# Four small edits of order in a fused linear-attention and gated-FFN kernel: fill-in matmuls of the head, one conversion step, the place of a square, the place of a joint insertion

## The chip, the cores and the metric

The kernel runs on one core of a Trainium2 chip. A core has five engines that run side by side, each with a queue of its own that it works through strictly in order: TensorE (PE, the matmuls, with its weight loads shown as PEld), VectorE (DVE), ScalarE (ACT), GpSimd (POOL) and SyncE (SP, which here only issues DMAs). They meet by semaphores. The metric is device time in microseconds for one execution; lower is better. An instruction that waits for another engine blocks everything behind it in its own queue, and this is what most of this document turns on.

## The reference: what is computed

For 8 batches, 8 heads, 576 positions and head size 64:

```
kv  = einsum('bhsd,bhse->bhde', k, v)
out = einsum('bhsd,bhde->bhse', q, kv)
x   = out / sqrt(mean(out*out, -1) + 1e-6) * g_norm      -> (4608, 512)
y   = (sigmoid(x @ w_gate) * (x @ w_val)) @ w_out        d_ff = 1536
```

All arithmetic is in float32. The three weight matrices arrive as float64, so the kernel gets them as 64-bit words and turns these into float32 itself.

## The kernel before, in words

**Chunks.** The 4608 tokens are worked off in nine chunks of 512 (`G`). Chunk 0 uses ordinary matmuls: eleven blocks of `plain` (line 630, matmuls at L618) after one block that is woven into the head, then the second layer (`second`, L853). Chunks 1 to 8 use a fast matrix multiplication with 26 products for each 4-by-4 grid of blocks (`PRODUCTS1`, `PRODUCTS2`): `first_layer_fast` (L977) runs 78 products, numbered p = 0 to 77, in three groups of 26, and `second_layer_fast` (L1079) runs 26 more with three matmuls each. Each product adds into one of up to eleven named regions; there are five PSUM banks for them, handed out and taken back in the queue `free`.

**Head.** The first four pairs of heads (batch 0) go through `attention` before chunk 0. Their steps are named in a string, `order` (L651), and issued in that order on all engines: `KVn` (matmuls, L299), `KVOn` (DVE copy, L303), `Qn` (transposes on PE, L309), `QOn` (ACT copy, L314), `Un` (matmuls, L326), `SQn` (ACT square, L331), `SUMn` (DVE, L335), `ROOTn` (ACT, L339), `NORMn` (DVE, L343 and L345), `Xn` (transposes on PE, L353), `XOn` (ACT, L362). Between them stand `warmN`: N matmuls of 128 by 128 into a bank that nobody reads (L671). In float32 each such matmul is two instructions in the profile. Their operand is `ident`, the identity that GpSimd makes first (masks.py:197 and 199). `wN` issues loads of weights and `cU.S`, `aU.S` are steps of a conversion.

**Conversion.** A unit u of weights (18 in all: units 0 to 11 for the first layer, 12 to 17 for the second) is turned into float32 by five DVE steps `s0` to `s4` (L195, L210, L222, L226, and L233 or L235) and two ACT steps: `a0` (L200) runs behind `s0`, and `s2` (L222) needs it; `a1` (L215) runs behind `s1`, and `s3` needs it. `s4` and `s2` also issue loads for a later unit on SP. In chunk 0 the next step is taken whenever `CV` stands in the string `places` (L827), at a place counted in matmuls of chunk 0 (eight to a block); an `s0` or `s1` brings its ACT step with it. During the second layer of chunk 0 three of four matmuls take one step each.

**The end of a block of chunk 0.** Each block's sigmoid (`gate`, ACT, L623) and its product with the other half (`end`, DVE, L626) are put off by `late` and issued at places 0 and 2 of the next block. At a place, `late` comes before the steps of `places`.

**Joint insertions.** Batches 1 to 7 are attended four pairs of heads at a time (`feed`), in two runs for each batch. A run's matmuls (`u_mm`, L450, and in front of the first run `kv_mm`, L389 and L400) are put between products of the fast layer as one block: the joint insertion. It lands in the three-bank tile `at` and in one lent bank. `u_square` (`q0`, `q1` in the strings) copies the lent piece over (L456), gives the bank back, and squares the whole (L459), both on ACT. Sums (`s00`, L462), root (`r0`, L465) and norms follow. The strings at L518 to L523 give, for each step, the product p behind which it is issued; the first string is for chunk 1 (`b == 2`), the second for chunk 2 (`b == 3`), the third for chunks 3 to 6. Behind a product come first its own sums and copies (`combine`, L943 for a copy on ACT, L947 for sums on DVE), then the steps of the string.

One dependence matters for the change: in the list of products, region B is copied out by ACT behind product i = 5 of each group of 26, and product i = 6 adds into that region, so it must wait for the copy:

```
("A", 24, 14, "o4=C"),  ("C", 26, 16, "o3=B o1=A"),  ("B", 25, 19, "o1=o1+B")     i = 4, 5, 6
```

Of the kernel before, what the change touches and what calls it, by code (L numbers as in the profile page):

```python
# [10 lines left out]
FP32 = mybir.dt.float32  # L11
# [9 lines left out]
def kernel(  # L21
# [11 lines left out]
    nc = tc.nc  # L33
# [4 lines left out]
    P = 128  # L38
# [34 lines left out]
    const = ctx.enter_context(tc.tile_pool(name="const", bufs=1))  # L73
# [75 lines left out]
    def load_unit(u, halves=(0, 1)):  # L149
        if u >= len(units):  # L150
            return
        kind, f = units[u]
        if 0 in halves:
            staged[u] = raw.tile([P, 2, DM], I64, tag="st", name="st", bufs=NST)
        st = staged[u]
        for i in halves:
            if kind == "gv":
                src = (moe_w_gate, moe_w_val)[i].rearrange("(m p) f -> p m f", p=P)[:, :, P * f:P * f + P]
                nc.sync.dma_start(out=st[:, i].rearrange("p (m f) -> p m f", m=NMT), in_=src)
            else:  # L160
                nc.sync.dma_start(out=st[:, i], in_=moe_w_out[P * (f + i):P * (f + i) + P, :])
# [7 lines left out]


    EXP_OFF = 896
    one = const.tile([P, 1], FP32, name="one")
    nc.vector.memset(one, 1.0)
    exp_off = const.tile([P, 1], FP32, name="exp_off")
    nc.vector.memset(exp_off, -EXP_OFF * 2.0 ** 23)

# [83 lines left out]
    w1 = const.tile([P, N3, 4 * NMT, 2, P], FP32, name="w1")  # L260
    w2 = const.tile([P, NFT, DM], FP32, name="w2")
    ident = const.tile([P, P], FP32, name="ident")
# [111 lines left out]
    def feed(b):  # L374
# [132 lines left out]
        u0, u1 = heads_run(0), heads_run(1)  # L507
# [5 lines left out]
        if b == 1:  # L513
# [2 lines left out]
        names = f"t00 t01 t10 t11 u0 q0 s00 s01 r0 {n_.format(0)} x00 x01 u1 q1 s10 s11 r1 {n_.format(1)}".split()  # L516
        steps_ = dict(zip(names, t0 + t1 + u0 + u1[:-2]))
        where = """0:t00 5:t01 25:u0 26:q0 28:t10 30:s00,s01 33:t11 35:r0 36:n00 37:n01 39:n02 40:n03 42:n04 43:n05 44:n06  # L518
                   51:x00 52:x01 53:u1 56:q1 57:s10,s11 60:r1 62:n10,n11 63:n12 65:n13 66:n14 68:n15 69:n16""" if b == 2 else """
                   5:t00 8:t01 25:u0 29:t10 30:q0 33:s00,s01 36:r0 39:t11 41:n00 47:n01 51:x00,x01 54:u1  # L520
                   56:q1,s10,s11 61:r1 64:n10 66:n11""" if b == 3 else """
                   3:t00 7:t01 25:u0 28:t10 30:q0,s00,s01 37:r0 39:t11 47:n00,n01 53:x00,x01 54:u1
                   56:q1,s10,s11 60:r1 61:n10 63:n11"""  # L523
        first = [(int(w_.split(":")[0]), steps_[x]) for w_ in where.split() for x in w_.split(":")[1].split(",")]
        return kv, first, u1[-2:]
# [53 lines left out]
    def bank(i):  # L579
        return (psum_mm if i < 2 else psum).tile([P, 512], FP32, tag=f"mm{i}", name="mm")  # L580
# [19 lines left out]
    warm, pair_kv = bank(0), bank(1)  # L600
# [29 lines left out]
    def plain(c, u, ps, steps_at):  # L630
# [18 lines left out]


    order = """  # L651
        w1 w2 warm8 KV0 Q0 KVO0 QO0 warm4 U0 SQ0 KV1 Q1 SUM0 ROOT0 KVO1 QO1 NORM0 warm3 U1 SQ1 X0 XO0 SUM1 ROOT1
        c0.0 a0.0 c0.1 a0.1 NORM1 warm11 X1 XO1 c0.2 KV2 Q2 KVO2 QO2 c0.3 c0.4 w3 warm3 U2 SQ2 KV3 Q3 SUM2 ROOT2 KVO3 QO3
        NORM2 b0.0.0 U3 SQ3 b0.1.0 X2 XO2 c1.0 SUM3 ROOT3 a1.0 c1.1 a1.1 NORM3 b0.0.1 b0.1.1 b0.0.2 X3 XO3 b0.1.2
        c1.2 c1.3 c1.4 w4 b0.0.3 b0.1.3
    """
# [1 line left out]
    for token in order.split():  # L658
        name = token.rstrip("0123456789.")
        n = [int(i) for i in token[len(name):].split(".")]  # L660
        f = n[0]
        if name == "b":
            blk = blk or Plain(0, F_ORDER[0], (warm, pair_kv))
            blk.mm(n[1], n[2])
        elif name in ("c", "a"):
            conversion[f][name][n[1]]()
        elif name == "w":
            load_unit(f)
        elif name == "warm":
            for _ in range(f):  # L670
                nc.tensor.matmul(warm[:, 0:P], ident, ident, start=True, stop=True)  # L671
        else:
            a[f][steps[name]]()
            if token == f"Q{NE - 1}":
                first_ctx.__exit__(None, None, None)
                hp = ctx.enter_context(tc.tile_pool(name="hp", bufs=1))
                h_main = [hp.tile([P, 4 * NT, P], FP32, name=f"h{j}") for j in range(N3)]
                h_more = hp.tile([P, N3, 3 * NT, P], FP32, name="h_more")
# [122 lines left out]
    def w1_form(c, j, part, v):  # L801
        if c == 1:
# [10 lines left out]
    w1_more[1] = [more[:, i] for i in range(10, 18)] + [sgs[-1][:, GH * i:GH * i + GH] for i in range(2)]  # L813
    spare_sg = sgs.pop()
    batch1, second_batch = feed(1), feed(2)
    named = {"LL": lambda: load_late(1), "LL2": lambda: load_late(2), 
             "W0": lambda: w1_sums(0), "W1": lambda: w1_sums(1),
# [6 lines left out]
    for i, which in enumerate("ab"):  # L824
# [3 lines left out]
        1:CV,CV 2:CV,Q0 4:CV,CV 5:CV,CV 6:CV,LL 7:CV,CV 10:CV,CV 11:Q1 15:CV 16:CV,CV 17:t00  # L828
        18:CV,CV 19:t01 22:CV,CV 25:CV 26:CV,CV 29:au,LL2 30:CV
        31:asq 32:CV,t10,as0,as1,art 34:arc,CV,an0 35:CV 36:CV,t11,an1 37:an2 38:CV 40:CV,CV 41:CV,ax0  # L830
        43:ax1 44:bu 46:CV,W0 47:bsq,ASIDE 48:CV,CV 50:CV,bs0 52:CV,CV 54:bs1 55:CV,CV,brt,D 57:CV,CV 58:CV 60:CV,brc
        62:bn0,bn1 63:bn2 64:CV 65:CV,CV,CV 66:CV,CV 67:CV 71:bx0 72:CV 74:W1 75:bx1
        80:CV,CV,CV,CV,CV 84:CV 87:CV
    """
    at_place = {}
    for some in places.split():
# [311 lines left out]
    X1 = (18, 19, 20, 21, 22, 22, 23, 23, 24, 24, 25, 26, 28, 30, 31, 33, 35, 37)  # L1148
# [59 lines left out]
```

## Time and profile before

| what | value |
|---|---|
| median of three runs | 999.95 us (999.59 to 1000.1) |
| profiled execution: its own time | 1001.39 us |
| profiled execution: its span | 999.6 us |
| PE busy | 992.4 us (99%) |
| DVE / ACT / POOL busy | 719.1 / 343.0 / 616.2 us |
| head, until PE runs on without a break | 0 to 33.1 us |
| first layer of chunk 0 | 33.1 to 116.2 us |
| second layer of chunk 0 | 116.2 to 158.1 us |
| chunk 1 | 158.1 to 262.0 us |
| chunks 2 to 6 | 106.3 us each, to 793.7 us |
| chunks 7 and 8 | 101.0 us each |

The span runs from the first to the last instruction. A row of the timeline gives the start, the duration, the engine and source line, the operation with output and inputs, how many instructions were merged, and in brackets how long the engine stood idle before and what released it. Matmuls are pipelined, so the end of a row reaches past the start of the next; the distance of two starts says more than a duration.

### The profile page before, as it was taken

The numbers are of one execution on the slowest core, as the hardware profiler recorded it, in microseconds if no ns is written. First come the engines' busy times: TensorE is split into PE (matmuls) and PEld (weight loads), VectorE is DVE, ScalarE is ACT, GpSimd is POOL, SyncE is SP. The second block draws the span as 40 slices with busy tenths as digits, with TensorE's granted clock in tenths as the row PEclk, the third lists the DMA queues.
The fourth block names the chain that finished last, engine by engine and source line by source line (L and its number), as shares of the span: only waits on it lengthen the run. The fifth ranks groups of instructions, "written<-read, shape, count | busy, mean of one in ns | idle before, by whom it ended". The sixth has DMA issues, their size and how long they took to land.

```text
span 999.6 us, 16578 instructions
## 1 busy us (share of the span) xinstructions
PE 992.4 (99%) x5958; PEld 816.2 (82%) x5958; DVE 719.1 (72%) x1185; ACT 343.0 (34%) x621; POOL 616.2 (62%) x991
## 2 busy tenths in 40 slices
PE   8999999999999999999999999999999999999998
PEld 7455447888888888888888888888888888888887
DVE  4989999898758766784777576866587566755672
ACT  4566332561144213530344124511442123213320
POOL 0439997798259634865286708771686349744963
PEclk9999999999999999999999999999999999999999
DMA  9995515763889468746975677656854455444614
GB/s 270 275 262 176 174 53 142 220 225 104 289 277 276 158 190 272 205 159 198 280 226 161 187 221 260 176 172 188 282 179 145 152 182 203 158 148 165 215 51 123
DMA packets 149522, 194.96 MB, mean 195 GB/s; under 512 B 79840, under 2 KB 121696, under 8 KB 149440
## 3 DMA queue, kind: packets, MB, share of 16 engines
q0 software_dynamic: 22512, 116.41, 35.1%
q1 hardware_dynamic: 120848, 75.66, 26.7%
q10 hardware_dynamic: 6080, 1.84, 0.8%
q8 instruction: 47, 0.77, 0.3%
q14 instruction: 35, 0.29, 0.1%
HBM read 160.04 MB, written 25.56 MB: 186 GB/s over the span
## 4 chain that ended last, share of the span: by engine, by line
PE 93%; DVE 4%; issue 1%; ACT 1%; DMA 0%; SPq 0%; DVEq 0%; ACTq 0%
PE mm L977 54%; PE mm L1079 27%; PE mm L618 5%; PE mm L853 3%; PE at L450 2%; DVE cz L226 1%; DVE w L222 1%; DVE w L195 1%; PE at L400 1%; PE mm L400 1%; DVE cz L210 0%; DMA q<-in_q_dram 0%; PE two L326 0%; DVE w L235 0%; DVE h L626 0%
## 5 line engine op out<-in xcount | busy, mean ns | idle before, releaser
L977 PE MATMUL mm<-xs,w 128*128 128x256 f32 x1428 | 331.8, 380 | 0.0
L977 PEld LDWEIGHTS mm<-xs,w 128*128 128x128 f32 x1428 | 270.5, 190 | 37.9 <-ACT sg L943 1.2
L977 PE MATMUL mm<-xT,w 128*128 128x256 f32 x948 | 230.6, 380 | 0.0
L977 PEld LDWEIGHTS mm<-xT,w 128*128 128x128 f32 x948 | 179.5, 190 | 25.0 <-issue 0.5
L799 POOL DMA_DIRECT2D w<-kept x84 | 46.9, 559 | 203.6 <-PE mm L977 200.1
L947 DVE TENSOR_TENSOR sg<-sg,mm 128x512 f32<-128x512 f32 (+1 forms) x176 | 100.8, 599 | 75.1 <-PE mm L977 34.4
L1079 PE MATMUL mm<-w,h 128*128 128x256 f32 x630 | 142.8, 379 | 0.0
L1079 PEld LDWEIGHTS mm<-w,h 128*128 128x128 f32 x630 | 119.7, 190 | 16.3
L943 ACT COPY temps<-mm 128x512 f32<-128x512 f32 (+1 forms) x128 | 66.2, 540 | 184.7 <-PE mm L1079 94.7
L939 POOL TENSOR_TENSOR h<-h,sg 128x512 f32<-128x512 f32 x72 | 96.8, 1362 | 43.9 <-ACT sg L936 27.8
L752 POOL TENSOR_TENSOR h<-h 128x128 f32<-128x128 f32 x216 | 109.9, 521 | 16.6 <-DVE h_more L752 13.1
L1079 PE MATMUL mm<-w,h_more 128*128 128x256 f32 x474 | 108.2, 379 | 0.0
L936 ACT ACTIVATE sg<-sg 128x512 f32<-128x512 f32 x96 | 59.7, 630 | 127.3 <-DVE sg L947 127.3
L1079 PEld LDWEIGHTS mm<-w,h_more 128*128 128x128 f32 x474 | 90.1, 190 | 12.2
L943 ACT COPY sg<-mm 128x512 f32<-128x512 f32 (+1 forms) x112 | 56.5, 511 | 84.1 <-PE mm L1079 45.3
L752 POOL TENSOR_TENSOR h_more<-h 128x128 f32<-128x128 f32 x120 | 58.5, 491 | 34.8 <-DVE h L939 30.5
L947 DVE TENSOR_TENSOR temps<-temps,mm 128x512 f32<-128x512 f32 (+1 forms) x96 | 59.5, 620 | 27.1 <-PE mm L1079 16.8
L947 DVE TENSOR_TENSOR temps<-mm,temps 128x512 f32<-128x512 f32 (+1 forms) x64 | 39.8, 623 | 52.3 <-PE mm L1079 23.9
L618 PE MATMUL mm<-xT,w 128*128 128x512 f32 x176 | 77.2, 595 | 0.1
L943 ACT COPY h<-mm 128x512 f32<-128x512 f32 x48 | 28.1, 586 | 142.9 <-PE mm L977 142.9
L947 DVE TENSOR_TENSOR sg<-mm,sg 128x512 f32<-128x512 f32 (+1 forms) x64 | 39.7, 620 | 42.4 <-PE mm L1079 21.9
L618 PEld LDWEIGHTS mm<-xT,w 128*128 128x128 f32 x176 | 32.8, 190 | 40.0 <-issue 36.8
(154 smaller groups left out, 1298.1 us busy)
## 6 DMA issues: line engine op xcount, KB each, us to landing
w<-kept POOLq DMA_DIRECT2D x42, 896.0 KB, 5.1
w<-kept POOLq DMA_DIRECT2D x90, 384.0 KB, 4.5
w<-kept POOLq DMA_DIRECT2D x42, 768.0 KB, 5.0
out_dram<-sg SPq DMA_DIRECT2D x119, 64.0 KB, 1.7
q<-in_q_dram SPq DMA_DIRECT2D x96, 72.0 KB, 5.1
xT<-xTs SPq DMA_DIRECT2D x96, 72.0 KB, 4.6
st<-in_moe_w_gate_dram SPq DMA_DIRECT2D x12, 512.0 KB, 5.3
st<-in_moe_w_val_dram SPq DMA_DIRECT2D x12, 512.0 KB, 6.6
```

What stands on the lines that cost most here:

```text
L400: nc.tensor.matmul(ps[m][HD * g:HD * g + HD, e], mains[2 * m + g, "k"][:, c], mains[2 * m + g, "v"][:, c], start=(b == 2 and e == 0 and j ...
L450: nc.tensor.matmul(to[HD * e:HD * e + HD], qTs[HD * g:HD * g + HD, c:c + HD], kvq[HD * g:HD * g + HD, m, e], start=True, stop=True)
L618: nc.tensor.matmul(self.ps[i], w[("wg", "wv")[i], self.f][:, m, :], xT[self.c][:, m, :], start=(m == 0), stop=(m == NMT - 1), skip_group_c ...
L752: ops.append((eng, lambda v=v, x=x, sign=sign, y=y, eng=eng: eng.tensor_tensor(out=h_form(v, j), in0=h_form(x, j), in1=h_form(y, j), op=op ...
L799: nc.gpsimd.dma_start(out=granule(g)[:, 0:n], in_=kept1[g // NPA % N3, g % NPA][:, 0:n])
L853: nc.tensor.matmul(ps[t], gv[0, f][:, P * t:P * t + P], w["wo", f], start=(f == 0), stop=(f == NFT - 1), skip_group_check=True)
L936: nc.scalar.activation(out=o["o" + step[1]], in_=o["o" + step[1]], func=AF.Sigmoid)
L939: mult.tensor_tensor(out=o[x], in0=o[x], in1=o[y], op=ALU.mult)
L943: nc.scalar.copy(out=o[out_], in_=o[expr])
L947: tt(out=o[out_], in0=o[x], in1=o[y], op=ALU.add if sign == "+" else ALU.subtract)
L977: nc.tensor.matmul(regions[name][1][:, g], ws[:, g], xf[c][wv], start=(new and g == 0), stop=True, skip_group_check=True)
L1079: nc.tensor.matmul(regions[name][1], h_form(hv, j), ws[:, j], start=(used[i] and j == 0), stop=(j == N3 - 1), skip_group_check=True)
```

## The change

1. Head: the fill-in matmuls multiply a tile of ones with itself. That tile is set by one DVE memset of 128 by 128 (it was 128 by 1; the old name stays as its first column, the bias of `a0`). Their numbers change: 9 for 8 at the start, one more between `KV0` and `Q0`, 3 for 4 ahead of `U0`, one between `SQ0` and `KV1`, 14 for 11 ahead of `X1`.
2. Conversion in chunk 0: a third step at place 48, none at place 87; the steps in between each move up by one in the sequence. At place 48 the additional step is `s4` of unit 8 (L233).
3. Chunks 2 to 6: the square of the first run is issued at product 26, right behind the insertion at 25, instead of at product 30.
4. Chunk 1: the second run's insertion comes behind product 54 instead of 53.

In chunk 0 the order on DVE and ACT from the additional step on is, for the three blocks that the prediction speaks of (numbers in brackets are lines; u is the unit):

```
DVE before: ... [226 u8] [626] [233 u8] [462] [195 u9] ...
DVE after:  ... [226 u8] [233 u8] [626] [195 u9] [462] ...
DVE before: [222 u10] [498] [226 u10] [233] [195 u11] [210 u11] [626] [222 u11] [226 u11]
DVE after:  [222 u10] [226 u10] [498] [233] [195 u11] [210 u11] [222 u11] [626] [226 u11]
ACT before: [494 x18] [623] [200 u11] [215 u11] [623] [200 u12] [623] [215 u12]
ACT after:  [494 x18] [623] [200 u11] [215 u11] [200 u12] [623] [215 u12] [623]
```

The order on SP and on GpSimd stays as it was. The diff:

```diff
-    one = const.tile([P, 1], FP32, name="one")
-    nc.vector.memset(one, 1.0)
+    ones = const.tile([P, P], FP32, name="ones")
+    nc.vector.memset(ones, 1.0)
+    one = ones[:, 0:1]
...
-                   51:x00 52:x01 53:u1 56:q1 57:s10,s11 60:r1 62:n10,n11 63:n12 65:n13 66:n14 68:n15 69:n16""" if b == 2 else """
-                   5:t00 8:t01 25:u0 29:t10 30:q0 33:s00,s01 36:r0 39:t11 41:n00 47:n01 51:x00,x01 54:u1
+                   51:x00 52:x01 54:u1 56:q1 57:s10,s11 60:r1 62:n10,n11 63:n12 65:n13 66:n14 68:n15 69:n16""" if b == 2 else """
+                   5:t00 8:t01 25:u0 26:q0 29:t10 33:s00,s01 36:r0 39:t11 41:n00 47:n01 51:x00,x01 54:u1
                    56:q1,s10,s11 61:r1 64:n10 66:n11""" if b == 3 else """
-                   3:t00 7:t01 25:u0 28:t10 30:q0,s00,s01 37:r0 39:t11 47:n00,n01 53:x00,x01 54:u1
+                   3:t00 7:t01 25:u0 26:q0 28:t10 30:s00,s01 37:r0 39:t11 47:n00,n01 53:x00,x01 54:u1
...
-        w1 w2 warm8 KV0 Q0 KVO0 QO0 warm4 U0 SQ0 KV1 Q1 SUM0 ROOT0 KVO1 QO1 NORM0 warm3 U1 SQ1 X0 XO0 SUM1 ROOT1
-        c0.0 a0.0 c0.1 a0.1 NORM1 warm11 X1 XO1 c0.2 KV2 Q2 KVO2 QO2 c0.3 c0.4 w3 warm3 U2 SQ2 KV3 Q3 SUM2 ROOT2 KVO3 QO3
+        w1 w2 warm9 KV0 warm1 Q0 KVO0 QO0 warm3 U0 SQ0 warm1 KV1 Q1 SUM0 ROOT0 KVO1 QO1 NORM0 warm3 U1 SQ1 X0 XO0 SUM1 ROOT1
+        c0.0 a0.0 c0.1 a0.1 NORM1 warm14 X1 XO1 c0.2 KV2 Q2 KVO2 QO2 c0.3 c0.4 w3 warm3 U2 SQ2 KV3 Q3 SUM2 ROOT2 KVO3 QO3
...
-                nc.tensor.matmul(warm[:, 0:P], ident, ident, start=True, stop=True)
+                nc.tensor.matmul(warm[:, 0:P], ones, ones, start=True, stop=True)
...
-        43:ax1 44:bu 46:CV,W0 47:bsq,ASIDE 48:CV,CV 50:CV,bs0 52:CV,CV 54:bs1 55:CV,CV,brt,D 57:CV,CV 58:CV 60:CV,brc
+        43:ax1 44:bu 46:CV,W0 47:bsq,ASIDE 48:CV,CV,CV 50:CV,bs0 52:CV,CV 54:bs1 55:CV,CV,brt,D 57:CV,CV 58:CV 60:CV,brc
         62:bn0,bn1 63:bn2 64:CV 65:CV,CV,CV 66:CV,CV 67:CV 71:bx0 72:CV 74:W1 75:bx1
-        80:CV,CV,CV,CV,CV 84:CV 87:CV
+        80:CV,CV,CV,CV,CV 84:CV
```

## The prediction

> **What bounds the kernel.** I read the page's chain that ended last first, then the PE timeline stretch by stretch for starts that lie further apart than they need, then the waits of PE's weight loads, then the other engines around each late start. PE carries the span:
>
> ```profile
> PE 93%; DVE 4%; issue 1%; ACT 1%; DMA 0%; SPq 0%; DVEq 0%; ACTq 0%
> ```
>
> So an edit pays only where PE itself is late. That is in the head (busy 29.97 of its first 33.10 us) and in a few places behind it. The head, PE alone:
>
> ```profile
> 1.37 3.78 PE L671 MATMUL mm<-ident 128*128 128x128 f32 x16 [1.37 <-POOL ident masks.py:199]
> 5.08 1.55 PE L299 MATMUL mm<-v,k 96*64 96x64 f32 x24
> 6.82 1.19 PE L309 MATMUL two<-ident,q 96*128 96x96 f32 x6 [0.19 <-DMA q<-in_q_dram]
> 7.80 1.97 PE L671 MATMUL mm<-ident 128*128 128x128 f32 x8
> 9.70 1.29 PE L326 MATMUL two<-kvq,qTs 64*64 64x64 f32 x40
> 10.93 0.92 PE L299 MATMUL mm<-v,k 96*64 96x64 f32 x24
> 11.78 0.71 PE L309 MATMUL two<-ident,q 96*128 96x96 f32 x6
> 12.33 0.86 PE L671 MATMUL mm<-ident 128*128 128x128 f32 x6
> ```
>
> The same work is slow at first and fast later: KV 1.55 then 0.92, Q 1.19 then 0.71, fill-ins 0.213 us apart then 0.112. TensorE runs at half speed until about 10.8 us. And U0 (9.70) starts a whole us after its input is ready (the copy L314 runs 8.05 to 8.69), because four fill-ins stand before it.
>
> The weight loads show the two other places that the change touches:
>
> ```profile
> PEld mm L853 <- DVE w L235: 1.7, 2, 1.0
> PEld mm L977 <- ACT sg L943: 1.4, 6, 0.2
> ```
>
> L853: at 123.10 and 130.37 PE waits for a converted unit. The L853 matmuls start at 116.21 and are 0.429 apart; 32 of them need 13.73 us, but the third unit starts after 14.16, and each of the two waits is followed by one start that is 0.10 late: 0.53 in all.
>
> L977: the six waits are one each in chunks 1 to 6, six products behind an insertion. Chunk 3, PE and then ACT:
>
> ```profile
> 397.05 4.59 PE L977 MATMUL mm<-xs,w 128*128 128x256 f32 x20
> ```
> ```profile
> 397.99 1.13 ACT L459 ACTIVATE sqs<-at 128x1152 f32<-128x1152 f32 x1
> 399.01 1.07 ACT L943 COPY sg<-mm 128x512 f32<-128x512 f32 x2
> ```
>
> The square holds up the copy of region B until 399.6, just when product i = 6 wants to add into it. Twenty matmuls at 0.216 plus the 0.17 of a row's tail are 4.48; the row has 4.59, so the wait costs 0.10.
>
> **The change, part by part.** The sum is made against the profiled execution's own span, 999.6; it lay 0.35 below the median of the runs shown (999.95; with the profiler on, the execution itself took 1001.39). I subtract from the median.
>
> *Head.* A memset of 128 by 128 took 0.20 on POOL, one of 128 by 1 0.06 on DVE; taking 0.20 (same shape), ones are there at 0.81 + 0.20 and PE starts at 1.06 instead of 1.37. Two more instructions at 0.213 put KV0 at 5.2 (5.08 before); its operands no longer wait for anything. The pair behind KV0 (0.43) lies in the gap 6.5 to 6.82, in which PE waits for q. So PE works from 1.06 on with no gap above 0.15, where before 0.14 and about 0.4 were free between 4.9 and 6.8. I take it that full speed comes before Q0, since before it came at the end of the first stretch as dense as this (7.0 to 10.8). Then: Q0 at 6.82 (its DMA binds) for 0.71, copy 0.04 later for 0.64, U0 at 8.25; the three fill-ins (0.86 with tail, from 7.38) are through by then. From a fast U's start to its square is 0.88 (13.54 to 14.42): SQ0 at 9.13 instead of 11.07, 1.94 earlier. From there the chain is ACT and DVE (SUM0, ROOT0, QO1, U1), unchanged; the fill-in behind SQ0 (0.22) hides there: U0 to KV1, Q1 and three fill-ins end at 11.4, U1 is due at 11.6. Fourteen fill-ins from 12.95 take 28 x 0.112 = 3.1, to 16.1; X1 is due at 16.4. What could be late next is DMA: v of pair 3 lands at 11.19 + 8.5 = 19.7, KV3 is then due at 20.2, free. Unit 1's second half lands at 16.80 + 7.2 = 24.0, and L195 (25.25 before) would be due at 23.3: DVE loses 0.7 there, of which 0.5 is a wait for SQ3 anyway; I take off 0.14. Head: -1.8, and from 33.1 on everything (DMA loads too, since they are issued behind these steps) shifts together. Bounds: -0.25 if full speed comes no earlier (second rival); -1.94 if no load binds.
>
> *Square at product 26.* It runs at 394.4 to 395.7 in the chunk shown, where ACT is idle (1.99 before its next copy). That copy (region A, 0.59) ends at 396.3, product i = 4 that adds into A comes at 397.9; then B's copy is ready by 398.4, over 1 us early. The lent bank goes back to the end of the same queue, and F at i = 9 is the next to take one, as before. Chunk 1 has its first run in this very order, and its PE rows show no wait there. -0.10 in five chunks: -0.52. Bounds: 0 to -0.55.
>
> *Chunk 1's second run.* PE does the same work; the insertion ends 0.86 later (208.2), the square runs to 209.6 instead of 210.3, as the copy of C goes ahead of it, and B's copy ends at 210.2, before product i = 6 (210.83). Chunks 2 to 6 have their second run at 54 with no such wait. -0.10; bounds 0 and -0.10.
>
> *Conversion step.* This one decides the sign of what is left. The views are DVE and ACT from 96 us:
>
> ```profile
> 96.12 0.25 DVE L498 RECIPROCAL ms<-ms 128x18 f32<-128x18 f32 x1
> 96.29 1.57 DVE L226 SCALAR_TENSOR_TENSOR cz<-st,cz 128x1024 uint32<-128x1024 uint32 x1
> ...
> 101.74 0.68 DVE L626 TENSOR_TENSOR h<-mm,sg 128x512 f32<-128x512 f32 x1
> 102.34 1.21 DVE L222 SCALAR_TENSOR_TENSOR w<-st,w 128x1024 f32<-128x1024 uint32 x1
> ```
> ```profile
> 96.41 3.80 ACT L494 ACTIVATE sqs<-at,ms 128x64 f32<-128x64 f32 x18 [0.69 <-DVE ms L498]
> 99.96 0.73 ACT L623 ACTIVATE sg<-mm 128x512 f32<-128x512 f32 x1
> 100.70 1.15 ACT L200 ACTIVATE w<-w,one 128x1024 f32<-128x1024 uint32 x1
> ```
>
> The additional L233 (1.27 at 82.75) goes into a DVE gap of 1.77 (80.38 to 82.14, waiting for PE), so the steps behind it come 1.27 earlier. But each L626 now stands one step later, and so does the reciprocal: behind L226, at 96.12 - 1.27 + 1.57 = 96.42. The 18 norms, L623 and L200 on ACT follow it, 0.3 later than before: L200 of unit 11 ends at 102.15. DVE stands before L222 of that unit at 102.34 - 0.60 - 1.27 = 100.47, waits 1.7, starts it at 102.2, and only then does L626 (0.60): L226 at 103.92, 0.45 later than before. The gain is gone. At unit 12 it happens again: L623 now stands behind L200 of unit 12, which waits for DVE's L195; that L195 comes at 107.2 and ends at 108.3, L200 109.5, L623 110.0, while DVE, past the transpose and L210, stands at L626 from 109.6. Another 0.45. So unit 13 is ready 0.9 later, unit 14 too, and PE, which waited for both already, goes on at 130.37 + 0.9. Unit 15 was 2 us early (ready 135.1 + 1.2, due 137.2) and stays so. Taken: +0.9. Bounds: -0.53 (all waits gone) and +1.3 (the reciprocal and both L626 each cost 0.4 more, since DVE's steps of one kind take 0.68 or 1.22 here, as POOL works beside them or not).
>
> Sum: -1.8 - 0.52 - 0.10 + 0.9 = -1.5; 999.95 - 1.5 = 998.4.
>
> **The rivals.** First, *the conversion step does what its gap suggests*: if the reciprocal or the norms come earlier than I work out, L222 never waits, both PE waits go: 999.95 - 1.8 - 0.62 - 0.53 = 997.0. For it: the 1.77 gap, and that DVE is back to back from 82 to 130. Against: the order of ACT's queue, which no shorter DVE step changes.
>
> Second, *full speed comes no earlier*. Then the extra pair puts Q0 at 7.0, three fill-ins for four bring U0 to 9.70 + 0.18 - 0.43 = 9.45, and only 0.25 is won: 999.95 - 0.25 - 0.62 + 0.9 = 1000.0. For it: KV0's small matmuls and Q0's transposes fill most of the stretch in question, and the start of 16 dense fill-ins, 3.6 us long, was not enough before. [...]
>
> Third, on the other side, *full speed comes only when X0 is through* (say 17.6). The Q1 stretch at half speed (1.4 for KV1, 1.0, and 1.6 for the fill-ins) puts U1 at 15.3 instead of 13.54, X0's end at 17.6, and fourteen fill-ins bring X1 to 20.9, 2.5 late: 999.95 + 2.5 - 0.62 + 0.9 = 1002.7. It decides once full speed comes after about 15 us. For it: 14 for 11 stand in front of X1. Against: PE is denser than before, when it came at 10.8.
>
> **How the numbers follow.** My forecast 0.52 (own range 997.7 to 999.1), first rival 0.25, second 0.15, third 0.05, the rest 0.03. A change of 0.2% is 2.0 us, about what a measurement of this kernel can tell from none: below 997.95 is faster, above 1001.95 slower. Faster: first rival 0.25 and the lower part of my own range, 0.15: 0.40. Slower: 0.06. Same: 0.54. The range from 996.8 to 1000.3 holds the first three.
>
> **What the profile will show.** Right: first row of PE near 1.06, Q0 0.71 long at 6.82, U0 near 8.25; no weight load of L977 waiting for L943 in chunks 1 to 6; on DVE a wait of L222 for L200 near 100 and of L626 for L623 near 108; the L853 waits grown to about 1.4. Wrong: Q0 near 1.2 long, or L853 without waits, or a new wait of L977.

## The result: slower by half a percent

The changed kernel takes 1005.32 us (median of six, 1003.63 to 1007.26) where the kernel before took 1000.03 beside it (median of six too, one of them a stray 3718.28); the ratio is 1.0053, 95% interval 1.0041 to 1.0065. I had forecast 998.4, with 996.8 to 1000.3 as the range. The profiled execution spans 1003.8 us and took 1005.61 itself; that of before spanned 999.6 and took 1001.39. Lines of the changed kernel are one higher than in the text above (L619 is the old L618).

The chain of work that ended last, by engine, in the changed kernel (before, it was "PE 93%; DVE 4%; issue 1%; ACT 1%; DMA 0%; SPq 0%"):

```profile
PE 94%; DMA 3%; SPq 2%; issue 1%; DVE 1%; ACT 0%; ACTq 0%; DVEq 0%
```

What has grown on it is DMA (3%) and the issuing of DMAs (2%): loads that were early enough before now set the end of stretches. The head shows it first. PE's timeline of the changed kernel, rows as in the prediction:

```profile
1.06 4.21 PE L672 MATMUL mm<-ones 128*128 128x128 f32 x18 [1.06 <-DVE eps L277]
5.54 1.25 PE L300 MATMUL mm<-v,k 96*64 96x64 f32 x24 [0.27 <-DMA v<-in_v_dram]
...
7.14 0.69 PE L310 MATMUL two<-ident,q 96*128 96x96 f32 x6
7.66 0.86 PE L672 MATMUL mm<-ones 128*128 128x128 f32 x6
8.55 0.81 PE L327 MATMUL two<-kvq,qTs 64*64 64x64 f32 x40
...
17.23 0.74 PE L354 MATMUL two<-ident,sqs 128*128 128x128 f32 x5 [0.20 <-DVE sqs L346]
...
19.36 0.69 PE L310 MATMUL two<-ident,q 96*128 96x96 f32 x6 [0.54 <-DMA q<-in_q_dram]
...
23.17 0.69 PE L310 MATMUL two<-ident,q 96*128 96x96 f32 x6 [0.68 <-DMA q<-in_q_dram]
```

Up to X1 it goes the way that I forecast, but not all of it: Q0 is 0.69 long instead of 1.19, U0 comes at 8.55 (9.70 before, 8.25 in the forecast), X1 at 17.23 (18.38 before, 16.4 in the forecast). KV0 waits 0.27 for v and Q1, in the part left out, 0.35 for q. Then Q2 and Q3 wait for q, and at 24.7 us only 0.13 of the 1.15 is left. The page's list of DMAs says the same of the staged units: the last number is the median time from issue to landing, first of before, then of after.

```profile
st<-in_moe_w_gate_dram SPq DMA_DIRECT2D x12, 512.0 KB, 5.3
st<-in_moe_w_val_dram SPq DMA_DIRECT2D x12, 512.0 KB, 6.6
```
```profile
st<-in_moe_w_gate_dram SPq DMA_DIRECT2D x12, 512.0 KB, 7.1
st<-in_moe_w_val_dram SPq DMA_DIRECT2D x12, 512.0 KB, 7.8
```

The rest of the loss sits in three places. The waits of PE's weight loads (total, times, longest), first before, then in the changed kernel:

```profile
PEld mm L618 <- issue: 36.8, 154, 0.2
...
PEld mm L977 <- issue: 0.5, 2, 0.2
```
```profile
PEld mm L619 <- issue: 38.7, 154, 2.1
...
PEld mm L978 <- issue: 3.0, 4, 1.4
...
PEld mm L854 <- DVE w L236: 1.3, 2, 0.9
```

"Issue" means that nothing is named that they waited for. The longest of these of L618 was 0.2 before; now there is one of 2.1, and L978 has 3.0 in four. The first of them, PE's timeline at the end of the insertion of chunk 0, first before, then in the changed kernel:

```profile
62.51 0.22 PE L450 MATMUL mm<-kvq,qTs 64*64 64x64 f32 x2
62.66 4.56 PE L618 MATMUL mm<-xT,w 128*128 128x512 f32 x10
```
```profile
61.93 1.21 PE L451 MATMUL at<-kvq,qTs 64*64 64x64 f32 x66 [0.49 <-ACT kvq L414]
...
62.98 0.23 PE L451 MATMUL mm<-kvq,qTs 64*64 64x64 f32 x2
65.19 1.98 PE L619 MATMUL mm<-xT,w 128*128 128x512 f32 x4 [1.98 <-issue]
```

PE stands still for 2 us. The like happens at 506.05 (0.93) and at 719.00 (1.20). The row at 61.93 shows one more new wait: the insertion's matmuls (L451) wait for L414, the copy on ACT that hands them `kvq`.

Start by start against the kernel before, PE's shift is -0.13 at 24.7 us; +0.60 for the wait for L414; +2.05 for the gap behind it; -0.22 at the two L854 waits; -0.10 in chunk 1 and -0.52 in chunks 2 to 6 for the moved squares and insertion; +1.09 and +1.36 for the other two gaps: +4.1 in all.

### The profile page after: what moved, and what is told of

Read it like the earlier page. It is cut to its first block, busy times and chain, and to the rows that moved or that the text cites. A ratio compares the mean times of both kernels' runs of the same rounds, so it can differ in the third digit from the quotient of the medians.

```text
span 1003.8 us, 16604 instructions
## 1 busy us (share of the span) xinstructions
PE 991.9 (99%) x5968; PEld 816.2 (81%) x5968; DVE 717.4 (71%) x1185; ACT 343.4 (34%) x621; POOL 616.0 (61%) x991
## 4 chain that ended last, share of the span: by engine, by line
PE 94%; DMA 3%; SPq 2%; issue 1%; DVE 1%; ACT 0%; ACTq 0%; DVEq 0%
PE mm L978 54%; PE mm L1080 27%; PE mm L619 5%; PE mm L854 4%; PE at L451 2%; DMA q<-in_q_dram 1%; DMA h_more<-in_v_dram 1%; PE at L619 1%; DMA st<-in_moe_w_val_dram 1%; PE at L401 1%; SPq L132 1%; PE mm L401 1%; DMA g_col<-in_g_norm_dram 0%; SPq L93 0%; SPq L159 0%
## 5 line engine op out<-in xcount | busy, mean ns | idle before, releaser
L978 PE MATMUL mm<-xs,w 128*128 128x256 f32 x1428 | 331.4, 379 | 1.2 <-issue 1.2
L978 PEld LDWEIGHTS mm<-xs,w 128*128 128x128 f32 x1428 | 270.9, 190 | 38.3 <-issue 1.4
L978 PE MATMUL mm<-xT,w 128*128 128x256 f32 x948 | 230.7, 380 | 0.9 <-issue 0.9
L978 PEld LDWEIGHTS mm<-xT,w 128*128 128x128 f32 x948 | 179.6, 190 | 26.1 <-issue 1.6
L1080 PEld LDWEIGHTS mm<-w,h 128*128 128x128 f32 x630 | 119.6, 190 | 16.4 <-POOL h L940 0.2
L619 PE MATMUL mm<-xT,w 128*128 128x512 f32 x176 | 77.2, 595 | 2.1 <-issue 2.0
L619 PEld LDWEIGHTS mm<-xT,w 128*128 128x128 f32 x176 | 32.8, 190 | 42.1 <-issue 38.7
```

What stands on the lines that cost most here:

```text
L619: nc.tensor.matmul(self.ps[i], w[("wg", "wv")[i], self.f][:, m, :], xT[self.c][:, m, :], start=(m == 0), stop=(m == NMT - 1), skip_group_c ...
L978: nc.tensor.matmul(regions[name][1][:, g], ws[:, g], xf[c][wv], start=(new and g == 0), stop=True, skip_group_check=True)
L1080: nc.tensor.matmul(regions[name][1], h_form(hv, j), ws[:, j], start=(used[i] and j == 0), stop=(j == N3 - 1), skip_group_check=True)
```

## The experiments

Each ratio compares all executions of the two kernels that ran side by side, with its 95% interval in brackets. It is not the quotient of two medians: in e4 these would give 1.0021 and in e1 1.0081.

**First set: which part, and is it the number of instructions?** A load of PE's instructions shows in the trace as a DMA queue of its own, "instruction", with 47 packets of 16384 bytes. PE has 12183 instructions in the kernel before (weight loads, matmuls and waits, counted from 0), so I read a packet as a block of 256 instructions of 64 bytes. The three gaps lie at instructions 1217, 6593 and 9409, which all leave 193 when divided by 256. The change adds five fill-ins, that is 20 PE instructions. So my first theory was that the count had put a block's end behind an insertion; the rival was the loads.

`e1_head`: only the new head (tile of ones and numbers of fill-ins).

```diff
-    one = const.tile([P, 1], FP32, name="one")
+    ones = const.tile([P, P], FP32, name="ones")
...
-        w1 w2 warm8 KV0 Q0 KVO0 QO0 warm4 U0 SQ0 KV1
+        w1 w2 warm9 KV0 warm1 Q0 KVO0 QO0 warm3 U0 SQ0 warm1 KV1
...
-        NORM1 warm11 X1
+        NORM1 warm14 X1
```


> Only the head of the change (tile of ones, 34 fill-ins instead of 29); conversion, square and second run as before. Theory 1, blocks of code: PE's queue gets its instructions in blocks of 256, and with 20 more instructions in the head a block's end falls right behind an insertion; then the three stalls of the changed kernel (2.0, 0.9 and 1.2 us) come here too, at the same instruction numbers 1217, 6593 and 9409: 1003 to 1006 us. Theory 2, loads: a faster head lets the loads fall behind and this costs time later: slower too, by 0.5 to 2 us, at places that follow a load. Theory 3, the conversion step costs the time: within 1 us of before.

Measured: 1007.87, ratio 1.0066 [1.0051, 1.0081]. The gaps are there, at the same three instructions: the head carries the whole loss. (It is above the ratio of the whole change, 1.0053, but the intervals overlap.)

`e2_rest`: the other three edits, with the old head.

```diff
-        48:CV,CV 50:CV,bs0
+        48:CV,CV,CV 50:CV,bs0
...
-        25:u0 29:t10 30:q0 33:s00,s01
+        25:u0 26:q0 29:t10 33:s00,s01
...
-        52:x01 53:u1
+        52:x01 54:u1
```

> Everything but the head (29 fill-ins of ident as before; conversion step, square and second run as changed). Theory 1: no stall for code, and what the rows of the changed kernel show for these edits (-0.52 for the squares, -0.10 for the second run, -0.2 at the two waits of L853): 998.9 to 999.6. Theory 3: the conversion step costs 0.9, or more without the late PE that covered it there: 1000.3 or above.

Measured: 999.91, ratio 0.9998 [0.999, 1.0007], no gap. The five squares give 0.10 to 0.11 each in its trace.

`e3_fill34`: the kernel before with five more fill-ins on the old tile, 34 as in the change.

```diff
-        QO1 NORM0 warm3 U1
+        QO1 NORM0 warm4 U1
...
-        NORM1 warm11 X1
+        NORM1 warm15 X1
```


> The kernel before with five fill-ins of ident more and nothing else (15 for 11 ahead of X1, 4 for 3 ahead of U1); the head is no faster. Theory 1: the 20 instructions alone bring the stalls: 1003 to 1006 us. Theory 2: the loads are issued as before, X1 comes 0.25 later: 1000.0 to 1000.4.

Measured: 1001.15, ratio 1.0012 [1.0002, 1.0022]; no long gap (0.5 or more) in the profiled execution, which took 1001.25 and so no longer than that of before. The count alone makes a small part, and this trace does not show where.

`e4_after29`: the changed kernel with the old count of 29.

```diff
-        NORM1 warm14 X1
+        NORM1 warm9 X1
```


> The changed kernel with 9 instead of 14 fill-ins ahead of X1, so with 29 in all like before. Theory 1: from X1 on the ends of the blocks lie where they lay before, the stalls for code are gone, and what is left of the gains shows: 998.0 to 999.4, faster than before. Theory 2: the faster head still upsets the loads: 1001 or above. Theory 3: 1000 or above.

Measured: 1001.88, ratio 1.0012 [1.0003, 1.002]; no long gap, but the wait for L414 is there (1.03), and the loads are as late as in the change. Neither theory alone holds: these gaps do not come without the count, and something in the new head makes the loads late.

**Second set: the addresses.** The records of single DMA packets showed what the page does not: the packets of k, v and q take longer in the kernels with the tile of ones. The 256-byte packets (q) of the first 34 us, mean: 18.8 ns before, 18.6 in e2, 26.4 after, 24.1 in e4; the 1536-byte packets (k and v) 84.7 before and 103.3 after. In the allocation of these programs the new tile, 512 bytes of a partition instead of 32, moves every tile behind it by 480 bytes. Before, k, v and q began on multiples of 512 (k at 148992); after, none does (149472). The tiles that hold weights lie off such multiples in both kernels, and the staged units, at the upper end, do not move at all.

`e7_after_64`: the changed kernel with eight unused columns on the tile of ones, so that everything behind it moves by 512 bytes instead of 480.

```diff
-    ones = const.tile([P, P], FP32, name="ones")
+    ones_wide = const.tile([P, P + 8], FP32, name="ones")
+    ones = ones_wide[:, 0:P]
```


> The changed kernel with the tile of ones 136 columns wide instead of 128 (544 bytes of a partition instead of 512; only the first 128 columns are set and read). In the kernel before, the tiles of k, v, q and the ring of weights begin at SBUF addresses that are multiples of 512 bytes; the tile of ones moves all of them by 480 bytes, to an odd multiple of 32; with 136 columns they move by 512. Theory 'addresses' (the loads got slower because their tiles no longer begin on a multiple of 64 bytes; the late loads took back the head's gain, held up L414 and delayed the fetch of PE's instructions): the 256-byte packets of the first 34 us go back from 26.4 ns to 18.8 in the mean, X1 and the first steady matmul keep the gain of over 1 us, no wait of L451 for L414 over 0.3, no gap of 1 to 2 us near 63, and the time comes near what I first forecast, 998 to 999.5. Theory 'ones' (PE's earlier and denser work slows the DMA, or the new order of loads does): packets stay near 26 ns, time 1004 to 1006. Theory 'blocks' (20 more instructions put a fetched block's end behind the insertion, whatever the loads do): gaps of 1 to 2 us at PE instructions 1217, 6593 and 9409 stay, time 1001 to 1003.

Measured: 999.72, ratio 0.9996 [0.9986, 1.0006]. Packets 18.4 ns, no wait for L414, one gap of 0.4 us left at 9409. Eight unused columns take the loss away.

`e8_before_32`: the kernel before with its tiles moved by 32 bytes.

```diff
-    one = const.tile([P, 1], FP32, name="one")
+    one_wide = const.tile([P, 9], FP32, name="one")
+    one = one_wide[:, 0:1]
```


> The kernel before with the tile one 9 columns wide instead of 1 and nothing else (its first column is what is read): all tiles behind it move by 32 bytes. Theory 'addresses': 256-byte packets of the first 34 us from 18.8 to about 24 to 28 ns, the loads of units 4 to 6 some 2 to 4 us later as in the changed kernel, time 1000.5 to 1003 (PE's blocks end elsewhere than in the changed kernel, so the long gaps may be missing). Theories 'ones' and 'blocks': as before, 999.8 within 0.4.

Measured: 1001.80, ratio 1.0021 [1.0012, 1.003]. Packets 24.6 ns; L451 waits for L414 0.67 more; loads of st 7.1 and 7.6 us. No gap at instruction 1217; one of 0.4 at 9409. In the profiled execution PE is 1.24 later than before at the end; where the rest of the 0.21% lies, this one trace does not show.

`e9_fill34_32`: e3 and e8 together. There is no tile of ones in it, and no earlier start of PE.

```diff
+    one_wide = const.tile([P, 9], FP32, name="one")
...
+        QO1 NORM0 warm4 U1
...
+        NORM1 warm15 X1
```

> The kernel before with both of the above: tiles moved by 32 bytes, and 34 fill-in matmuls with the old tile (15 ahead of X1, 4 ahead of U1). Without the shift of tiles this count of fill-ins gave 1001.15, and no long gap in the profiled execution. If a gap needs both a block's end behind the insertion and a late fetch, gaps of 1 to 2 us are back at PE instruction 1217 (near 62.7) and perhaps at 6593 and 9409, and the time is 1002.5 to 1006, with no tile of ones and no earlier start of PE in the kernel. If the long gaps come from the new head itself: 1001 within 0.7, no gap over 0.5.

Measured: 1007.09, ratio 1.0075 [1.0059, 1.0091]. PE's timeline in e9:

```profile
63.20 0.23 PE L451 MATMUL mm<-kvq,qTs 64*64 64x64 f32 x2
65.50 5.83 PE L619 MATMUL mm<-xT,w 128*128 128x512 f32 x9 [2.08 <-issue]
```

The gap is back, at 1217, and so are those at 6593 and 9409. Put side by side:

| ratio to before | tiles as before | tiles moved by 32 |
|---|---|---|
| 29 fill-ins | 1 | 1.0021 |
| 34 fill-ins | 1.0012 | 1.0075 |

Apart the two cost 0.33% in sum, together 0.75%. The kernels with the tile of ones and the new head make the same table: 0.9993 with 29 fill-ins and the tiles in place (e10, below), 0.9996 with 34 and in place (e7), 1.0012 with 29 and moved (e4), 1.0053 with 34 and moved (the change).

Why together: the trace gives for each block when its packet landed and when PE ran its first instruction. In the 13 cases with a long gap (three each in the changed kernel, e1 and e9, two each in e14 and e15) that instruction follows the landing by 1.22 to 1.58 us, and in none of the twenty kernels profiled here does any block follow sooner. With the count alone (e3, e7) the three blocks follow by 1.33 to 1.70, so they come only just in time. A block's packet starts about when PE enters the block before it: 0.2 us later in the median of all blocks, though from 3.7 earlier to 4.6 later in nine of ten. Those that start over 1.5 us later mostly meet full DMA engines (a busy share of 0.8 or more until the packet starts in 233 of 280 cases). The windows from 58 to 62 us, the last two columns being the DMA engines' busy share and GB/s, before and after:

```profile
58.00:60.00 2.00, 2.00 (x37) 1.07 (x37) 1.39 (x3) 1.67 (x2) 0.00 (x0) 1.00 1.09 380
60.00:62.00 2.00, 2.00 (x90) 1.93 (x88) 1.88 (x2) 1.06 (x3) 1.11 (x2) 1.00 0.12 34
```
```profile
58.00:60.00 2.00, 2.00 (x41) 1.16 (x41) 1.19 (x2) 0.46 (x1) 0.00 (x0) 1.00 1.09 346
60.00:62.00 2.00, 1.51 (x54) 1.38 (x53) 1.39 (x3) 2.00 (x4) 1.20 (x2) 1.00 1.10 350
```

Before, the loads were through at 60 and the packet started at 60.27; after, they ran until past 62 and it started at 62.63, landed at 63.75, and PE went on at 65.19. PE had entered the block before at 59.96 and 59.64. That block holds the insertion, and PE works it off in 6.7 us in the kernel before, in 2.9 in e7, where no ordinary matmuls fill its end; a block of the fast layer's matmuls alone lasts 27. e8 has the same late packet (62.69 to 63.84) and no gap, because with 20 instructions less the next block begins ten long matmuls further on, at 67.26.

`e6_sq`: the square and chunk 1's second run alone.

```diff
-        25:u0 29:t10 30:q0 33:s00,s01
+        25:u0 26:q0 29:t10 33:s00,s01
...
-        52:x01 53:u1
+        52:x01 54:u1
```

> The square at product 26 and chunk 1's second run one product later, alone (places of tiles and instruction counts unchanged). All theories: five chunks 0.08 to 0.11 shorter each and 0.11 in chunk 1, together 0.5 to 0.65: 999.2. If the scheduler's other choices undo it: 999.8.

Measured: 999.42, ratio 0.9995 [0.9987, 1.0004]; in the trace 0.10 to 0.11 for each of chunks 2 to 6, as worked out. Its head is that of the kernel before, instruction by instruction, and yet:

```profile
5.08 1.39 PE L299 MATMUL mm<-v,k 96*64 96x64 f32 x24
7.13 0.69 PE L309 MATMUL two<-ident,q 96*128 96x96 f32 x6 [0.66 <-DMA q<-in_q_dram]
7.65 1.08 PE L671 MATMUL mm<-ident 128*128 128x128 f32 x8
8.66 0.81 PE L326 MATMUL two<-kvq,qTs 64*64 64x64 f32 x40
```

Full speed before 7.1 us and U0 at 8.66, with the old fill-ins. In the profile that I predicted from, it came at 10.8.

**Third set: the change without its side effects.** `e10_after29_64`: the changed kernel with both corrections, 136 columns and 9 fill-ins ahead of X1.

```diff
-    ones = const.tile([P, P], FP32, name="ones")
+    ones_wide = const.tile([P, P + 8], FP32, name="ones")
...
-        NORM1 warm14 X1
+        NORM1 warm9 X1
```

> The changed kernel with both suspected causes taken away: the tile of ones 136 columns wide, so that all tiles are on multiples of 64 bytes again, and 9 fill-in matmuls ahead of X1 instead of 14, so that PE has as many instructions as in the kernel before. If addresses and instruction blocks are the whole of the loss, what is left is the change as I forecast it: no gap over 0.5 us at PE instructions 1217, 6593, 9409, squares -0.1 in each of six chunks, time 998.7 to 999.4 (the head's early clock is in most timed executions of the kernel before already, since their median lies 1.4 us under the profiled one with the late clock). If something else of the new head costs time: 1000 to 1002.

Measured: 999.69, ratio 0.9993 [0.9983, 1.0002], no gap. This is the change as I had costed it: not 998.4 but 999.7, and above what I expected of this run. The waits in e10:

```profile
PEld mm L620 <- issue: 37.3, 156, 0.2
...
PEld mm L855 <- DVE w L237: 1.8, 2, 1.0
```

`e11_before_st64`: the kernel before with the staged units moved from 196576 to 196544, a multiple of 64, by way of `exp_off`, which goes to a pool at the upper end; `one` is 9 columns wide, so that the tiles behind it stay where they are (the other tiles at the upper end move with the units).

```diff
+    off = ctx.enter_context(tc.tile_pool(name="off", bufs=1, side="right"))
     raw_ctx = tc.tile_pool(name="raw", bufs=1, side="right")
-    exp_off = const.tile([P, 1], FP32, name="exp_off")
+    exp_off = off.tile([P, 1], FP32, name="exp_off")
```


> The kernel before with the staged units (st) on multiples of 64 bytes as well: in the kernel before they begin at an odd multiple of 32 (196576). exp_off goes to a pool of its own at the upper end, which moves the pool of st down by 32 bytes; one is 9 columns wide, so that nothing else moves. Theory 'addresses': the 1024-byte packets of the units' loads (51 ns where they run alone, at 24 to 28 us) go to 46, the loads come 10% sooner, and the waits of L195 for st get shorter; PE waits there for little, so 999.3 to 999.8. If the address counts for q, k and v alone (short rows): packets at 51, 999.8.

Measured: 999.64, ratio 0.9991 [0.9982, 1.0]; the 1024-byte packets at 24 to 28 us stay at some 51 ns. A multiple of 64 does nothing for them.

`e12_after29_st64` is e10 with that diff, `e13_sq_st64` is e6 with it.

> e10 and e11 together: the changed kernel with 29 fill-ins and all tiles, the staged units too, on multiples of 64 bytes. Theory 'addresses': the best of them so far, 998.4 to 999.2. Otherwise as e10.

> The kernel before with the square at product 26, chunk 1's second run one product later, and the staged units on multiples of 64 bytes: head, fill-ins and conversion steps as in the kernel before. 0.5 to 0.6 less than e11: 998.8 to 999.3. If the staged units' addresses give nothing: as the square edit alone, 999.4.

Measured: 999.47, ratio 0.999 [0.998, 0.9999], and 999.42, ratio 0.9992 [0.9982, 1.0001]. e12 is the one kernel whose interval lies below 1, by a hair.

**Fourth set: instruction number or place?** `e14_half_0` and `e15_half_32`: ten of the 34 fill-ins are cut into twenty of 64 columns, 40 instructions more; tiles as before, and moved by 32.

```diff
-        NORM1 warm11 X1
+        NORM1 warm5 half20 X1
...
+                nc.tensor.matmul(warm[:, 0:64], ident, ident[:, 0:64], start=True, stop=True)
```


> The kernel before with 34 fill-ins' worth of columns, of which ten are cut into twenty of 64 columns: 40 more PE instructions for the same columns, 60 more than in the kernel before, tiles at their old addresses. Theory 'blocks': the gap belongs to an instruction number, not to a place in the work. A block's end (number 1217) then falls 40 instructions earlier, in the middle of the insertion of chunk 0, which runs at some 14 ns an instruction; the fetched block can be used at about 62.8, as in e3, the insertion comes to number 1217 near 62.2: a gap of 0.3 to 0.8 us there, at an earlier matmul of the insertion, and the like may show in chunks 3 and 5. Time 1001 to 1003. Rival 'place' (something at the insertion's last product makes PE wait, whatever the numbers): no gap, or one at the same matmul as in e9, time as e3, 1001.2.

> The same with all tiles moved by 32 bytes. Theory 'blocks': the gap of 2.15 us that e9 has at number 1217 is at number 1217 again, so 40 instructions earlier in the work (among the insertion's own products, before its last matmul), 2.2 to 3 us long; at 6593 and 9409 1.5 to 2.5 us. Time 1006 to 1010. Rival 'place': the gap stays at the matmul where e9 has it, so at a number near 1257.

Measured: 1005.16, ratio 1.0051 [1.0034, 1.0068], and 1008.36, ratio 1.008 [1.0065, 1.0095]. Three misses: the halves take as long as whole fill-ins (0.11 each), so X1 comes some 2 us later, and e14 is slower than I expected; there is no gap at 1217, since the block's packet now started ahead of the crowded stretch (54.74 and 58.21); and there is none at 9409. The gap in chunk 4 tells number from place. Its insertion in e15:

```profile
502.28 1.15 PE L451 MATMUL at<-kvq,qTs 64*64 64x64 f32 x63
506.07 0.37 PE L451 MATMUL at<-kvq,qTs 64*64 64x64 f32 x3 [2.63 <-issue]
```

In e9 the gap of this chunk lay behind the insertion, among the matmuls of the fast layer; now it splits the insertion itself, and it is at instruction 6593 again. The same in e14 (503.75, instruction 6593), and both have one at 3777, which also leaves 193. The gap belongs to the number, not to the place. And e14 has its tiles in place, with packets of 19.4 ns:

```profile
PEld at L450 <- issue: 3.9, 7, 1.9
```

So a long gap can come without the slow packets, when the block ends inside the insertion; the slow packets are one way to it, not the only one.

**Fifth set: which multiple?**

`e16_before_64` and `e17_before_128`: as e8 with 64 and 128 bytes.

```diff
-    one_wide = const.tile([P, 9], FP32, name="one")
+    one_wide = const.tile([P, 24], FP32, name="one")
...
+    one_wide = const.tile([P, 40], FP32, name="one")
```

> The kernel before with all tiles behind one moved by 64 bytes instead of 32 (the tile one is 24 columns wide). If a multiple of 64 bytes is enough: 256-byte packets 18.8 ns, time as before, 999.8 within 0.5. If packets must begin on a multiple of their own 256 bytes: packets 22 to 28 ns as with 32, time 1000.9 to 1003.

> The same with 128 bytes. If 64 is enough: 18.8 ns and 999.8 within 0.5. If 256 is what counts: packets 22 to 28 ns, 1000.9 to 1003. [...]

Measured: 1002.52, ratio 1.0019 [1.0011, 1.0028], and 1000.35, ratio 1.0001 [0.9992, 1.0009]. The 256-byte packets take 24.4 and 23.3 ns: neither multiple is enough. A multiple of 256 is: a tile of q holds two heads in turn, 256 bytes each, so half of its packets begin 256 past a multiple of 512, and in the kernel before nine in ten of all take 20 ns or less. In time, 64 costs what 32 does, and 128 nothing that can be measured, against my expectation; why its slower packets cost nothing I have not settled.

`e18_before_st256`: as e11, the staged units on a multiple of 256 (196352).

```diff
-    exp_off = off.tile([P, 1], FP32, name="exp_off")
+    exp_off = off.tile([P, 56], FP32, name="exp_off")[:, 0:1]
```

> The kernel before with the staged units on multiples of 256 bytes (196352; with 64 in e11 their packets stayed at 51 ns). If 256 is what counts for the 1024-byte packets: 46 ns where they run alone (24 to 28 us), and the loads of the units come some 10% sooner; PE hardly waits for them, so 999.2 to 999.8. If their 51 ns come from elsewhere (the rows they are read from): 51, and 999.7.

Measured: 1000.09, ratio 0.9992 [0.9983, 1.0001]; the 1024-byte packets at 24 to 28 us take 46.0 ns, and 46.3 in e19; in the kernels with the units off such a multiple they take 50.4 to 53.5 there. But from 44 to 48 us those of the kernel before take 46 too, with the units at the same place, so the place alone does not set their time. The units land 4.9 and 5.7 us after their issue, which decides nothing: e7, with the units not moved, has 5.1 and 5.9. The time hardly moves either.

`e19_after29_st256`: e10 with that diff.

> The changed kernel with 29 fill-ins, tiles at multiples of 512 as in the kernel before, and the staged units on multiples of 256: as e12 or up to 0.4 less, 999.0 to 999.5.

Measured: 999.44, ratio 0.9994 [0.9985, 1.0002].

## Why the prediction was wrong, point by point

**"A memset of 128 by 128 took 0.20 on POOL"**, and "ones are there at 0.81 + 0.20 and PE starts at 1.06". PE does start at 1.06. The memset, on DVE, took 0.17. But its time was the only price that I put on the tile. Its size moved every tile behind it off the multiples of 256 bytes: from before to e8, 32 bytes alone make 0.21%; from e10 to e4, the tiles' place makes 0.19%. No rival of mine had this mechanism. The 256-byte packets took 18.4 to 19.5 ns in the twelve kernels with q on a multiple of 256, and 23.2 to 26.4 in the other eight; why a packet takes longer off such a multiple, no run shows.

**"Two more instructions at 0.213"**, "fourteen fill-ins from 12.95 take 28 x 0.112". The fill-ins were costed by their time on PE, and that was right: X1 is not held up by them. Not costed was that they are 20 more instructions in PE's stream, so that the blocks of 256 end elsewhere. With the late loads this turned into gaps of 0.93 to 1.98 us: from e4 to the changed kernel 1.0012 to 1.0053. With fast loads the same 20 instructions cost next to nothing behind the new head (0.9993 in e10, 0.9996 in e7) and 0.12% behind the old (e3). Of the 47 packets of 16384 bytes, three came too late for PE in the changed kernel, and none in the kernel before.

**"What could be late next is DMA."** The right place, but with the durations of before. I put -0.14 on it; in the trace it took 1.0 of the head's 1.15, and 0.6 more at L414 later. I had copied landing times from a kernel whose addresses the change does not keep. In e10, with the tiles in place, Q2 and Q3 do not wait and PE is 1.56 ahead of the kernel before at 23.25.

**"I subtract from the median."** This failed even without the side effects. The head's -1.8 was worked out against a profiled execution that took 1001.39 itself and had full speed only at 10.8. The median execution takes 1.4 less. In e6 the same head has full speed before 7.1, its profiled execution took 999.25, and PE is 1.52 ahead of the profile of before at 24 us; e10, with the new head, is 1.56 ahead there. So in these two profiles the new head won 0.04 over an old one that is fast early. The median already contains most of what I counted as the gain; e10 measures what is left, 999.69. I compared the span with the median (0.35) where its own time should have stood (1.44), and that 1.44 is most of the head's term of 1.8.

**"I take it that full speed comes before Q0."** Right in all seven kernels that I profiled with ones (U0 between 7.91 and 8.55). But with the old tile it came early in six of thirteen as well (U0 at 7.82 to 8.66), so the tile at best makes likelier what was already about as likely as not. Nor does it keep the speed: in e19 PE waits 1.99 for X1 behind only nine fill-ins, the granted clock from 20 to 22 us is 0.50, and this execution took 1001.88. In one of those with the old tile full speed came only after U1: the third rival's mechanism, with the old fill-ins. e16, PE's timeline:

```profile
10.87 1.35 PE L327 MATMUL two<-kvq,qTs 64*64 64x64 f32 x40
...
13.62 1.22 PE L310 MATMUL two<-ident,q 96*128 96x96 f32 x6
...
16.11 1.32 PE L327 MATMUL two<-kvq,qTs 64*64 64x64 f32 x40
```

**Squares, -0.52, and chunk 1, -0.10.** Right. In the changed kernel chunks 2 to 6 gain 0.08 and four times 0.11, 0.52 in sum; in chunk 1 it is 0.09 by the shift of PE. Chunk 3 of the changed kernel, ACT: the square is through well before the copy of region B, which starts at 399.85 as soon as A's is done.

```profile
396.94 1.13 ACT L460 ACTIVATE sqs<-at 128x1152 f32<-128x1152 f32 x1
397.97 0.58 ACT L944 COPY h<-mm 128x512 f32<-128x512 f32 x1
399.36 0.59 ACT L944 COPY h<-mm 128x512 f32<-128x512 f32 x1 [0.81 <-PE mm L978]
399.85 0.59 ACT L944 COPY sg<-mm 128x512 f32<-128x512 f32 x1
```

**Conversion step, +0.9.** The mechanism was right, the size was not. I had L222 of unit 11 wait 1.7 for L200. DVE, first L226 of that unit before, then the changed kernel:

```profile
103.47 1.74 DVE L226 SCALAR_TENSOR_TENSOR cz<-st,cz 128x1024 uint32<-128x1024 uint32 x1
```
```profile
104.34 1.42 DVE L223 SCALAR_TENSOR_TENSOR w<-st,w 128x1024 f32<-128x1024 uint32 x1 [1.64 <-ACT w L201]
105.68 0.68 DVE L627 TENSOR_TENSOR h<-mm,sg 128x512 f32<-128x512 f32 x1
106.28 1.21 DVE L227 SCALAR_TENSOR_TENSOR cz<-st,cz 128x1024 uint32<-128x1024 uint32 x1
```

And the second wait, of L626 for L623 near 108, which I put at 0.45, is 0.38 in e10:

```profile
108.17 0.69 DVE L628 TENSOR_TENSOR h<-mm,sg 128x512 f32<-128x512 f32 x1 [0.38 <-ACT sg L625]
```

What I missed is that the steps behind a wait got shorter: L226 of that unit 1.21 here and 1.74 before. Nor do the 0.68 and 1.22 of my upper bound go by POOL alone: in the kernel before, with POOL busy all through both, L210 took 0.68 at 93.85 and 1.22 at 100.59. PE is later by 0.19 in e10 at the two waits of L853, not by 0.9, and in the changed kernel, with its other delays, earlier by 0.22.

**The rivals.** All three were about the moment of full speed and the conversion step. The slower one, 1002.7, rested on full speed behind X0, which did not happen in the changed kernel. The loss came through two things that I read from no row of the kernel before, but that the diff shows: a tile of another size ahead of all others, and another number of instructions.

## What to carry to other kernels

A tile made 480 bytes larger moved every tile allocated behind it here, and with 512 instead the ratio went from 1.0053 to 0.9996 (e7): look up where the targets of DMAs begin before and after, and pad to a multiple of 256 bytes, where the 256-byte packets took 18.4 to 19.5 ns. Count the instructions that an edit adds to PE (20 here), and ask which dense stretch will then hold the end of a block of 256, and whether the DMA engines are full just before (a share of 1.10 here, and a gap of 1.98). And when the profiled execution is longer than the median, find out which of its stretches makes the difference before a gain in that stretch is taken off the median.

## What the runs showed of the hardware

- Addresses: packets of 256 bytes into SBUF took 18.4 to 19.5 ns in the mean of the head where they began on a multiple of 256 (twelve kernels), and 23.2 to 26.4 where the tiles were moved by 32, 64, 128 or 480 bytes (eight kernels). For packets of 1024 bytes it is open: 46.0 against 50.4 to 53.5 in one stretch, 46 off the multiple in another.
- Instruction blocks: PE ran the first instruction of a block no sooner than 1.22 us after its packet landed, in any block of the twenty profiles. In the changed kernel a packet started 2.99 us after PE entered the block before at 59.64, with the DMA engines' share at 1.10 from 60 to 62; in the kernel before it was 0.31, with a share of 0.12.
- Speed after a gap: behind the gap of 2.08 us in e9 the next L619 matmuls were 0.85 us apart instead of 0.43, until 69.9, which cost another 1.7; the granted clock from 66 to 68 us was 0.54. e1 has the same behind its gap of 1.9 (0.50), and e15 behind the one of 2.63 (0.50 from 506 to 508), but the changed kernel behind its own 1.98 has not (1.00). So in e9 the gap cost nearly twice its length, and in the changed kernel no more than its length.
- The moment of full speed moved with one and the same stream of instructions: with the old fill-ins from 1.37 us on, it came between 5 and 18 us in thirteen profiled kernels. It is read from the starts (fill-ins 0.213 us apart, then 0.112, in the kernel before); the granted clock is 1.00 there from 0 to 10.8 us as well as from 10.8 to 12.4, so what sets the moment is not shown. Between the profiles of before (late) and e6 (early) it is worth 1.52 us at 24 us. Of the 132 executions of the kernel before that ran beside these experiments 73 lie below 1000.2, and 25 in a second heap from 1001 to 1001.6; I take these to be the two moments, but that is not shown, and e11 took 1000.95 with full speed before U0 (8.34).
